# Retention attention, expert layer and closing layer on one core: another place for the split of the closing weights, and another order of work in the closing groups

## The chip, the cores and the metric

The kernel runs on one NeuronCore of a Trainium2 chip. The core has five engines that run side by side, each with its own queue in program order: TensorE (PE, matrix products into PSUM), VectorE (DVE), ScalarE (ACT), GpSimd (POOL, which cannot read PSUM) and SyncE (SP, which here issues nearly all DMAs). An instruction that has to wait holds up everything behind it on its own engine. The metric is the device time of one launch in microseconds (us), as the median of several runs.

## The reference

Three layers follow one another on 1536 rows of 512 columns (2 batches of 768 positions, 8 heads of 64).

```
attention:  blocks of 64 positions, masked by powers of lam, with a carried key-value state
experts:    P = exp(x @ w_gate - max), 8 times scaled by row sums and column sums
            out += P[:, e] * (relu(x @ w1[e]) @ w2[e])        for e in 0..7,  w1: 512x1024, w2: 1024x512
closing:    h = x @ w_in;  g = h - tanh(h);  out = g @ w_out   w_in: 512x2048, w_out: 2048x512
```

Everything is float32. The launch converts nothing but the layout: the closing weights w_in and w_out reach the kernel as 64-bit words, and the kernel turns them into float32 itself.

## The kernel before, in words

Every product in float32 is made of three products of reduced operands: each operand is split into a high part (a rounded copy, made by ACT with an fp32r output) and a low part (the source less the high part, made by DVE or POOL), and PE multiplies high by high, low by high and high by low. The helper is `split` (L174 to L178). The 512x512 products of first layers go by a scheme of seven products of sums of quarters instead of eight products of quarters; the quarters' sums are made on DVE and POOL beforehand, and the seven results are joined by DVE and ACT.

**The slots.** The expert layer runs in 64 slots (L819 to L868), each for a half of the rows and a sixteenth of all hidden columns. A slot has seven products into PSUM, `pal` four times, `pbl` once and `pbh` twice, each of six matmuls of 384 columns, and six `tiles` of the slot before, each of six matmuls of 512 columns. In the order of the code: product 1 into `pal`, which ACT copies to `sa` (L839); product 2 (`pbl`) and 5 (`pbh`); ACT copies `pbh` to `sa` (L845); product 6 onto `pal`, which must wait until L839 has read `pal`; ACT copies `pal` to `sb` (L848); three tiles of the slot before; product 7 onto `pal`, which must wait for L848; then DVE's sum `pah` (L855), the other three tiles, product 4 and product 3. `relu` (L674) makes the high part by ACT and the low part by DVE. Each tile is added by DVE to the accumulator `yacc` (L639). The PSUM bank of `pal` becomes the next slot's `pbh` when its `relu` is done.

Between these, four lists of small steps are run in every slot: `fd` after product 5, `fa` after L855, `fb` after the second three tiles, `fc` at the slot's end. They were filled by `put(list, slot, function, ...)` (L727 to L788). They hold the load (`w_load`, in `fc`), the quarter sums (`w_sum`, POOL, in `fa` of even slots) and the splits (`w1_split` in `fd` and `fa`, `w2_split` in `fb` of odd slots) of the next expert weights.

**The conversion of the closing weights.** The same lists hold `conv` (L560), which turns the 64-bit closing weights into float32 and stores their high and low parts in device memory (`wscr`) for later. There are 64 pieces of 128x256 words, 8 for each of the 8 parts of the layer, spread over slots 6 to 59; ten even slots take two pieces. For each piece: step 0 loads the words into `d` (`fc` of the slot before); step 1 (`fa`) has five DVE instructions (L576 to L583) and two of POOL (L584, L585), and writes the value `c`; step 2 (`fc`) has two of DVE (L587, L588) and then, at once, the split: ACT's high part `hl` (L176), POOL's low part (L178), and the store, which is put on a list and sent to SP when a later step calls `flush` in a later slot. A second piece of a slot uses `fd`, `fb` and the next slot's `fd` instead. The fourth piece of each part (p = 3) makes sums of quarters on POOL (L594, L595) and splits two of them at once, and in the next slot's `fa` two more (L607, L608). `block` (L553) rotates over three staging buffers `hl0` to `hl2`, `c` over five; a buffer `hl` of double width takes two pieces of w_out before its store.

**The closing groups.** From L936 on, 24 groups g run: three blocks of 512 rows times eight parts of 256 hidden columns. A group makes seven products of six matmuls of 256 columns into two PSUM banks `f0`, `f1` (each is one "unit" of 128x512), in the order 1, 2, 5, 6, 7, 3, 4. Between them `seconds` multiplies the finished units of earlier groups by w_out: unit 1 of group g-2 after product 2 and after product 6, unit 0 of group g-1 after product 3 and after product 4, two tiles at a time, each tile three matmuls of 512 columns. DVE and ACT join the products: `s1` (L942), DVE's L945 (after product 2; product 5 waits for it), L958, `s2` (L960, after product 6; product 7 waits for it), L978 and L980.

`unit(g, i, ...)` (L898) makes g = h - tanh(h) of a unit: ACT's square `t` (L908), ACT's `th` = tanh (L910), ACT's `q1`, `q2`, `mk` from `t` (L912 to L914); DVE's `w` = h*t (L916), `sub` = h - th (L918), the polynomial (L920, L921) and a predicated copy that chooses between polynomial and difference (L923); then ACT's high part (L926) and DVE's low part (L928). ACT and DVE take turns on the same PSUM bank in the order of the code, also where both only read.

**The turn from slots to groups.** At the end of the last slot the accumulators are transposed (`turn`, L681) and split for the first closing block by seven `x2_step`s on DVE and ACT (L713, L787), before the last `relu` and the last six tiles, which are spread over group 0.

Of the kernel before, what the change touches and what calls it, by code (L numbers as in the profile page):

```python
# [8 lines left out]
F32 = mybir.dt.float32  # L9
F32R = mybir.dt.float32r  # L10
BF16 = mybir.dt.bfloat16
I32 = mybir.dt.int32
# [17 lines left out]
NQ = FF // 512  # L30
# [25 lines left out]
def kernel(  # L56
# [494 lines left out]
        stores.append((now[0], tag, lambda: nc.sync.dma_start(out=wscr[q][:, :, o:o + m], in_=t.bitcast(F32))))  # L551

    def block(q, o, src):  # L553
        tag = f"hl{count[1] % 3}"
        t = staged(tag, 256, f"hl{q}_{o}")
        count[1] += 1
        split(t[:, 0], t[:, 1], src, nc.gpsimd)
        store(q, o, t, tag)

    def conv(u, i, j):  # L560
        q, p = 2 * u + i // 8, i % 8
        flush()
        if j == 0:
            d = cp.tile([128, NC64, 2], I32, tag="d", name=f"d{u}_{i}")
            nc.sync.dma_start(out=d.rearrange("p n t -> p (n t)"),
                              in_=wio[u].bitcast(I32)[:, i * 2 * NC64:(i + 1) * 2 * NC64])
            c0 = cp.tile([128, NC64], I32, tag="c0", name=f"c0_{u}_{i}")
            box[q, p] = [d, c0]
            return
        if j == 1:  # L570
            box[q, p].append(cq.tile([128, NC64], I32, tag=f"c1_{count[0] % 5}", name=f"c1_{u}_{i}"))
            count[0] += 1
        d, c0, c1 = box[q, p]
        hi, lo, val = d[:, :, 1], d[:, :, 0], c1.bitcast(F32)
        if j == 1:
            nc.vector.tensor_scalar(out=c0, in0=hi, scalar1=3, scalar2=0x40000000,  # L576
                                    op0=ALU.logical_shift_left, op1=ALU.bitwise_xor)
            nc.vector.tensor_scalar(out=c1, in0=hi, scalar1=-0x80000000, scalar2=None, op0=ALU.bitwise_and)
            nc.vector.scalar_tensor_tensor(out=c0, in0=c0, scalar=0x7FFFFFFF, in1=c1,
                                           op0=ALU.bitwise_and, op1=ALU.bitwise_or)  # L580
            nc.vector.tensor_scalar(out=val, in0=lo.bitcast(U32), scalar1=2.0 ** -52,
                                    scalar2=None, op0=ALU.mult)
            nc.vector.tensor_scalar(out=lo, in0=c0, scalar1=-0x800000, scalar2=None, op0=ALU.bitwise_and)  # L583
            nc.gpsimd.tensor_tensor(out=val, in0=val, in1=lo.bitcast(F32), op=ALU.mult)  # L584
            nc.gpsimd.tensor_tensor(out=val, in0=val, in1=c0.bitcast(F32), op=ALU.add)  # L585
        elif j == 2:
            nc.vector.tensor_scalar(out=lo, in0=hi, scalar1=0x7FFFFFFF, scalar2=None, op0=ALU.bitwise_and)  # L587
            nc.vector.scalar_tensor_tensor(out=val, in0=lo.bitcast(F32), scalar=thr, in1=val,  # L588
                                           op0=ALU.is_ge, op1=ALU.mult)
            if p < 3:  # L590
                block(q, (0, 256, 1536)[p], val)
            elif p == 3:
                a11, a22 = (box[q, k][2].bitcast(F32) for k in (0, 2))
                nc.gpsimd.tensor_tensor(out=a22, in0=val, in1=a22, op=ALU.add)  # L594
                nc.gpsimd.tensor_tensor(out=val, in0=a11, in1=val, op=ALU.subtract)  # L595
                block(q, WI[5], a22)
                block(q, WI[7], val)
            else:
                if p % 2 == 0:
                    box[q] = staged("hl", 512, f"hl{q}_{p}")  # L600
                ht, lt_ = (halves(box[q][:, t])[:, :, 128 * (p % 2):128 * (p % 2) + 128] for t in range(2))
                split(ht, lt_, odds(val), nc.gpsimd)
                if p % 2:
                    store(q, 1792 + 512 * (p // 2 - 2), box[q], "hl")
        elif p == 3:
            a11, a12, a22 = (box[q, k][2].bitcast(F32) for k in range(3))
            nc.gpsimd.tensor_tensor(out=a11, in0=a22, in1=a11, op=ALU.subtract)  # L607
            nc.gpsimd.tensor_tensor(out=a12, in0=a12, in1=a11, op=ALU.subtract)  # L608
            block(q, WI[6], a11)
            block(q, WI[3], a12)  # L610

# [100 lines left out]

    def x2_step(b, n, eng):  # L713
        for i in X2[n][0]:
            x2_block(b, i, eng)
        if X2[n][1]:
            x2_sum(b, X2[n][1], eng)

# [57 lines left out]
    for s in range(lo_, hi_):  # L776
        more = s % 2 == 0 and (s - lo_) // 2 * extra // ((hi_ - lo_) // 2) != ((s - lo_) // 2 + 1) * extra // ((hi_ - lo_) // 2)
        for steps in (((fc, s - 1), (fa, s), (fc, s)), ((fd, s), (fb, s), (fd, s + 1)))[:1 + more]:
            for j, (f, at_) in enumerate(steps):
                put(f, at_, conv, n // (nconv // NQ), n % (nconv // NQ), j)  # L780
            if n % 8 == 3:
                put(fa, at_ + 1, conv, n // (nconv // NQ), n % (nconv // NQ), 3)
            n += 1
    assert n == nconv
    for k in range(KT):
        put((fb, fc)[k // 2], NS - 1, turn, 0, k)
    for n in range(7):  # L787
        put(fc, NS - 1, x2_step, 0, n, nc.vector)  # L788


    def product(ps, s, i, start):
# [75 lines left out]
        pend = pbh  # L867
        run(fc[s])  # L868
    relu(pend, 0, 1)
    tiles(NS - 1, range(TPE // 2))  # L870


    glos = [xp2.tile([128, 512], F32R, name=f"gl{i}") for i in range(2)]
    units = [xp2.tile([128, 512], F32, name=f"un{i}") for i in range(6)]
# [23 lines left out]
    def unit(g, i, *steps):  # L898
        if not 0 <= g < ng:
            return  # L900
        v = 2 * g + i
        for step in steps:
            if step == "t":
                tmp[v] = {n: kinds[n][v % len(kinds[n])] for n in kinds}
            e = tmp[v]
            h = ph[g, i]
            if step == "t":
                nc.scalar.activation(out=e["t"], in_=h, func=ACTF.Square)  # L908
            elif step == "th":
                nc.scalar.activation(out=e["th"], in_=h, func=ACTF.Tanh)  # L910
            elif step == "q":
                nc.scalar.activation(out=e["q1"], in_=e["t"], func=ACTF.Square, bias=bias[:, 0:1])  # L912
                nc.scalar.activation(out=e["q2"], in_=e["t"], func=ACTF.Square, bias=bias[:, 1:2], scale=LEAD ** 0.5)
                nc.scalar.activation(out=e["mk"], in_=e["t"], func=ACTF.Relu, bias=bias[:, 2:3])  # L914
            elif step == "w":
                nc.vector.tensor_tensor(out=e["w"], in0=h, in1=e["t"], op=ALU.mult)  # L916
            elif step == "sub":
                nc.vector.tensor_tensor(out=h, in0=h, in1=e["th"], op=ALU.subtract)  # L918
            elif step == "p":
                nc.vector.scalar_tensor_tensor(out=e["w"], in0=e["q1"], scalar=Q1 * Q1, in1=e["w"], op0=ALU.add, op1=ALU.mult)  # L920
                nc.vector.scalar_tensor_tensor(out=e["q2"], in0=e["q2"], scalar=LEAD * Q2 * Q2, in1=e["w"],  # L921
                                               op0=ALU.add, op1=ALU.mult)
                nc.vector.copy_predicated(out=e["q2"], mask=e["mk"].bitcast(U32), data=h)  # L923
            elif step == "hi":
                gs[g, i] = [hh[i][g % 2].rearrange("p t n -> p (t n)")[:, 0:512], glos[i]]
                nc.scalar.activation(out=gs[g, i][0], in_=e["q2"], func=ACTF.Copy)  # L926
            else:
                nc.vector.tensor_tensor(out=gs[g, i][1], in0=e["q2"], in1=gs[g, i][0].bitcast(F32), op=ALU.subtract)  # L928
# [7 lines left out]
    for g in range(ng):  # L936
# [1 line left out]
        ph[g, 0], ph[g, 1] = f  # L938
        c11, c12, c21, c22 = f[0][:, 0:256], f[0][:, 256:512], f[1][:, 0:256], f[1][:, 256:512]
        cproduct(g, c21, 1, True)  # L940
        unit(g - 1, 1, "t")
        nc.scalar.activation(out=s1, in_=c21, func=ACTF.Copy)  # L942
        cproduct(g, c11, 2, True)
        unit(g - 1, 1, "w")
        nc.vector.tensor_tensor(out=c11, in0=c11, in1=s1, op=ALU.add)  # L945
        unit(g - 1, 1, "th")
        unit(g - 1, 0, "hi")
        if g == 0:
            tiles(NS - 1, (3,))
        elif g == 1:  # L950
            turn(2, 0)
            turn(2, 1)
        seconds(g - 2, 1, (0, 1))
        unit(g - 1, 1, "sub")
        unit(g - 1, 0, "lo")
        unit(g - 1, 1, "q", "p")
        cproduct(g, c12, 5, True)
        nc.scalar.activation(out=s1, in_=c12, func=ACTF.Copy)  # L958
        cproduct(g, c21, 6, False)
        nc.scalar.activation(out=s2, in_=c21, func=ACTF.Copy)  # L960
        unit(g - 1, 1, "hi")
        b, j = g // NG + 1, g % NG - 1
        if b < NBLK and j >= 0:
            if b == 2 and j == 0:
# [5 lines left out]
            turn(2, 2)  # L970
            turn(2, 3)
        seconds(g - 2, 1, (2, 3))
        unit(g - 1, 1, "lo")
        for n, (_, _, p) in enumerate(loads):
            if p >= 0 and p == g - 2:
                w2_load(n)
# [1 line left out]
        nc.vector.tensor_tensor(out=c22, in0=c21, in1=s1, op=ALU.add)  # L978
        cproduct(g, c12, 3, False)
        nc.vector.tensor_tensor(out=c12, in0=c12, in1=s2, op=ALU.add)  # L980
        unit(g, 0, "t", "th", "w", "sub", "q", "p")
        if g == 0:
            tiles(NS - 1, (5,))
            w2_load(2)
# [7 lines left out]
                turn(1, k)  # L992
        seconds(g - 1, 0, (2, 3))
    g = ng - 1
    unit(g, 1, "t", "w", "th")
    unit(g, 0, "hi")
    second(g - 1, 1, range(TPB))
    unit(g, 1, "sub")
    unit(g, 0, "lo")
    unit(g, 1, "q", "p")  # L1000
    second(g, 0, range(TPB), (0, 1))
    second(g, 0, range(TPB), (2,))
    unit(g, 1, "hi", "lo")
# [48 lines left out]
```

## Time and profile before

| | |
|---|---|
| median of 3 runs | 1367.54 us (1367.46 to 1367.87) |
| the profiled execution's own time | 1367.77 us |
| its span in the profile | 1366.0 us |
| PE busy | 1268.4 us (93%) |
| DVE busy | 1000.9 us (73%) |
| ACT busy | 588.9 us (43%) |
| POOL busy | 525.1 us (38%) |
| chain that ended last | PE 51%, DVE 28%, ACT 10% |

The span is what the profiler saw from the first to the last instruction; the profiled execution's own time is 1.8 us longer. Busy time is an average over stages with different limits: the attention stage runs to about 100 us, the slots to about 1057 us, the groups to the end. A busy PE is not PE at its peak, since overlapping matmuls are counted to their modelled ends. In the rows below a bracket gives the engine's idle time before an instruction and what ended it.

### The profile page before, as it was taken

The numbers are of one execution on the slowest core, as the hardware profiler recorded it, in microseconds if no ns is written. First come the engines' busy times: TensorE is split into PE (matmuls) and PEld (weight loads), VectorE is DVE, ScalarE is ACT, GpSimd is POOL, SyncE is SP. The second block draws the span as 40 slices with busy tenths as digits, with TensorE's granted clock in tenths as the row PEclk, the third lists the DMA queues.
The fourth block names the chain that finished last, engine by engine and source line by source line (L and its number), as shares of the span: only waits on it lengthen the run. The fifth ranks groups of instructions, "written<-read, shape, count | busy, mean of one in ns | idle before, by whom it ended". The sixth has DMA issues, their size and how long they took to land.

```text
span 1366.0 us, 20272 instructions
## 1 busy us (share of the span) xinstructions
PE 1268.4 (93%) x7450; PEld 1146.2 (84%) x7450; DVE 1000.9 (73%) x1916; ACT 588.9 (43%) x1191; POOL 525.1 (38%) x692
## 2 busy tenths in 40 slices
PE   8999998798999999999999998999999789899897
PEld 6889887798898988988898998998889677777776
DVE  7978876576667777777777677777765677877776
ACT  5553333233333333333333333333332477777665
POOL 4943435244444545445444445444540021121000
PEclk9999999899999999999999999999999899999999
DMA  9210112212232322222222322222232364371651
GB/s 330 89 31 32 54 62 86 77 62 77 77 97 67 115 86 85 70 78 70 85 70 70 124 85 90 73 78 78 85 132 91 134 226 144 140 255 62 223 200 62
DMA packets 59283, 141.84 MB, mean 104 GB/s; under 512 B 5808, under 2 KB 24752, under 8 KB 59184
## 3 DMA queue, kind: packets, MB, share of 16 engines
q1 hardware_dynamic: 59040, 140.55, 30.7%
q8 instruction: 58, 0.95, 0.3%
q14 instruction: 41, 0.34, 0.1%
q10 hardware_dynamic: 144, 0.00, 0.0%
HBM read 114.32 MB, written 26.21 MB: 103 GB/s over the span
## 4 chain that ended last, share of the span: by engine, by line
PE 51%; DVE 28%; ACT 10%; issue 5%; POOL 3%; DMA 1%; DVEq 0%; SPq 0%; ACTq 0%; POOLq 0%
PE yq L624 9%; PE yq L625 9%; PE yq L626 9%; PE pal L797 5%; PE pal L800 5%; PE pal L799 5%; DVE yacc L639 3%; DVE un_raw L921 2%; DVE un L920 2%; DVE gl L928 2%; ACT un L910 2%; PE pbh L799 2%; PE pbh L800 2%; PE pbh L797 2%; DVE h1l L677 2%
## 5 line engine op out<-in xcount | busy, mean ns | idle before, releaser
L639 DVE SCALAR_TENSOR_TENSOR yacc<-yq,prob,yacc 128x512 f32<-128x512 f32 x336 | 238.8, 746 | 92.7 <-PE yq L626 92.6
L797 PE MATMUL pal<-xsh,w1h 128*128 128x384 f32 x384 | 131.0, 341 | 45.6 <-ACT sa L839 39.5
L624 PE MATMUL yq<-w2h,h1h 128*128 128x512 f32 x384 | 148.2, 386 | 5.7 <-DVE yacc L639 5.7
L625 PE MATMUL yq<-w2l,h1h 128*128 128x512 f32 x384 | 147.7, 385 | 0.0
L626 PE MATMUL yq<-w2h,h1l 128*128 128x512 f32 x384 | 147.4, 384 | 0.0
L624 PE MATMUL yq<-w2h,h0h 128*128 128x512 f32 x384 | 147.2, 383 | 0.0
L625 PE MATMUL yq<-w2l,h0h 128*128 128x512 f32 x384 | 146.9, 382 | 0.0
L626 PE MATMUL yq<-w2h,h0l 128*128 128x512 f32 x384 | 146.6, 382 | 0.0
L176 ACT ACTIVATE hl<-c 128x256 fp32r<-128x256 f32 x88 | 38.8, 441 | 209.6 <-DVE c L588 140.8
L800 PE MATMUL pal<-xsh,w1l 128*128 128x384 f32 x384 | 126.8, 330 | 0.0
L799 PE MATMUL pal<-xsl,w1h 128*128 128x384 f32 x384 | 126.6, 330 | 0.0
L797 PEld LDWEIGHTS pal<-xsh,w1h 128*128 128x128 f32 x384 | 73.2, 191 | 61.7 <-ACT sa L839 48.0
L178 POOL TENSOR_TENSOR w1l<-wsum,w1h 128x256 fp32r<-128x256 f32 x124 | 90.4, 762 | 89.4 <-ACT w1h L176 89.4
L178 POOL TENSOR_TENSOR hl<-c,hl 128x256 fp32r<-128x256 f32 x88 | 64.8, 744 | 148.6 <-ACT hl L176 110.7
L584 POOL TENSOR_TENSOR c<-c,d 128x256 f32<-128x256 f32 x64 | 47.5, 742 | 149.1 <-DVE d L583 144.5
L676 ACT ACTIVATE h1h<-pah 128x384 fp32r<-128x384 f32 x64 | 31.4, 491 | 167.2 <-PE yq L625 163.4
L677 DVE SCALAR_TENSOR_TENSOR h0l<-pbh,h0h 128x384 fp32r<-128x384 f32 x64 | 35.6, 557 | 89.3 <-ACT h0h L676 89.3
L178 POOL TENSOR_TENSOR w2l<-wraw,w2h 128x512 fp32r<-128x512 f32 x64 | 83.7, 1326 | 7.0 <-ACT w2h L176 7.0
L624 PEld LDWEIGHTS yq<-w2h,h1h 128*128 128x128 f32 x384 | 73.8, 192 | 13.1 <-DVE yacc L639 5.9
L624 PEld LDWEIGHTS yq<-w2h,h0h 128*128 128x128 f32 x384 | 73.7, 192 | 10.8
L626 PEld LDWEIGHTS yq<-w2h,h1l 128*128 128x128 f32 x384 | 73.8, 192 | 10.7
L625 PEld LDWEIGHTS yq<-w2l,h0h 128*128 128x128 f32 x384 | 73.6, 192 | 10.7
(228 smaller groups left out, 3636.1 us busy)
## 6 DMA issues: line engine op xcount, KB each, us to landing
wraw<-in_w SPq DMA_DIRECT2D x64, 512.0 KB, 5.0
d<-in_wio SPq DMA_DIRECT2D x64, 256.0 KB, 5.8
wscr<-hl SPq DMA_DIRECT2D x56, 256.0 KB, 3.8
w1h<-wscr SPq DMA_DIRECT2D x18, 768.0 KB, 4.5
w1l<-wscr SPq DMA_DIRECT2D x18, 768.0 KB, 5.9
w2h<-wscr SPq DMA_DIRECT2D x18, 512.0 KB, 3.8
w2l<-wscr SPq DMA_DIRECT2D x18, 512.0 KB, 4.7
wscr<-hl SPq DMA_DIRECT2D x16, 512.0 KB, 5.3
```

What stands on the lines that cost most here:

```text
L176: nc.scalar.activation(out=hi, in_=src, func=ACTF.Copy)
L178: eng.tensor_tensor(out=lo, in0=src, in1=hi.bitcast(F32), op=ALU.subtract)
L584: nc.gpsimd.tensor_tensor(out=val, in0=val, in1=lo.bitcast(F32), op=ALU.mult)
L624: nc.tensor.matmul(out=yp, lhsT=hi, rhs=pairs(w2h[q][:, i]), start=i == 1, stop=False)
L625: nc.tensor.matmul(out=yp, lhsT=hi, rhs=pairs(w2l[q][:, i]), start=False, stop=False)
L626: nc.tensor.matmul(out=yp, lhsT=lo, rhs=pairs(w2h[q][:, i]), start=False, stop=i == 0)
L639: nc.vector.scalar_tensor_tensor(out=y, in0=yp, scalar=prob[:, c, q // 4:q // 4 + 1], in1=y, op0=ALU.mult, op1=ALU.add)
L676: nc.scalar.activation(out=hi, in_=ps, func=ACTF.Relu)
L677: nc.vector.scalar_tensor_tensor(out=lo, in0=ps, scalar=0.0, in1=hi.bitcast(F32), op0=ALU.max, op1=ALU.subtract)
L797: nc.tensor.matmul(out=ps, lhsT=w1h[q][:, ws], rhs=pairs(xh[:, k]), start=start and k == 0, stop=False, skip_group_check=True)
L799: nc.tensor.matmul(out=ps, lhsT=w1h[q][:, ws], rhs=pairs(xl[:, k]), start=False, stop=False, skip_group_check=True)
L800: nc.tensor.matmul(out=ps, lhsT=w1l[q][:, ws], rhs=pairs(xh[:, k]), start=False, stop=k == 1, skip_group_check=True)
```

## The change

**Slots.** The split of a piece moves from step 2 to a new step 3, which is put in `fa` of the next slot (for a second piece: of the slot of its step 2). For p = 3, step 3 has only the POOL sums L594 and L595; step 4, a slot later, splits these two and makes the POOL sums L607 and L608; step 5, another slot later, splits those. `flush` sends all waiting stores at steps 0 and 2. `block` rotates over four buffers, `c` over seven.

**The turn.** The seven `x2_step`s are interleaved with the last relu and the first three of the last tiles, after them in part. The low parts of three of the seven operands go to POOL.

**Groups.** Order and place of the unit's steps change; no instruction is added or removed. `th` follows `t` at once for both units. L942 (`s1`) comes ahead of the unit's `t`. For unit 0 the second polynomial step and the predicated copy move into the next group, on both sides of L945; unit 1's predicated copy moves behind L980, and its high and low part into the work on the next unit 0.

```diff
-        tag = f"hl{count[1] % 3}"
+        tag = f"hl{count[1] % 4}"
...
-        flush()
+        flush(j in (0, 2))
...
-            box[q, p].append(cq.tile([128, NC64], I32, tag=f"c1_{count[0] % 5}", name=f"c1_{u}_{i}"))
+            box[q, p].append(cq.tile([128, NC64], I32, tag=f"c1_{count[0] % 7}", name=f"c1_{u}_{i}"))
...
+        elif j == 3:
             if p < 3:
                 block(q, (0, 256, 1536)[p], val)
             elif p == 3:
                 a11, a22 = (box[q, k][2].bitcast(F32) for k in (0, 2))
                 nc.gpsimd.tensor_tensor(out=a22, in0=val, in1=a22, op=ALU.add)
                 nc.gpsimd.tensor_tensor(out=val, in0=a11, in1=val, op=ALU.subtract)
-                block(q, WI[5], a22)
-                block(q, WI[7], val)
...
-        elif p == 3:
+        elif j == 4:
             a11, a12, a22 = (box[q, k][2].bitcast(F32) for k in range(3))
+            block(q, WI[5], a22)
+            block(q, WI[7], val)
             nc.gpsimd.tensor_tensor(out=a11, in0=a22, in1=a11, op=ALU.subtract)
             nc.gpsimd.tensor_tensor(out=a12, in0=a12, in1=a11, op=ALU.subtract)
+        else:
+            a11, a12 = (box[q, k][2].bitcast(F32) for k in range(2))
             block(q, WI[6], a11)
             block(q, WI[3], a12)
...
-            x2_block(b, i, eng)
+            x2_block(b, i, nc.gpsimd if i in (3, 7, 4) else eng)
...
+            at_ = (at_, at_ + 1)[f is fc]
+            put(fa, at_, conv, n // (nconv // NQ), n % (nconv // NQ), 3)
             if n % 8 == 3:
-                put(fa, at_ + 1, conv, n // (nconv // NQ), n % (nconv // NQ), 3)
+                for j in (4, 5):
+                    put(fa, at_ + j - 3, conv, n // (nconv // NQ), n % (nconv // NQ), j)
...
-    for n in range(7):
-        put(fc, NS - 1, x2_step, 0, n, nc.vector)
...
-    tiles(NS - 1, range(TPE // 2))
-
+    for t, steps in enumerate(((0, 1), (2,), (3,))):
+        for n in steps:
+            x2_step(0, n, nc.vector)
+        tiles(NS - 1, (t,))
+    for n in (4, 5, 6):
+        x2_step(0, n, nc.vector)
```

In `unit`, step "q" becomes "q1", "q2", "mk" and step "p" becomes "w1", "p2", "cp", each one instruction. The group's loop:

```diff
         cproduct(g, c21, 1, True)
-        unit(g - 1, 1, "t")
         nc.scalar.activation(out=s1, in_=c21, func=ACTF.Copy)
+        unit(g - 1, 1, "t", "th", "q1")
         cproduct(g, c11, 2, True)
-        unit(g - 1, 1, "w")
+        unit(g - 1, 0, "p2")
         nc.vector.tensor_tensor(out=c11, in0=c11, in1=s1, op=ALU.add)
-        unit(g - 1, 1, "th")
+        unit(g - 1, 0, "cp")
+        unit(g - 1, 1, "w", "sub")
         unit(g - 1, 0, "hi")
+        unit(g - 1, 1, "q2")
...
         seconds(g - 2, 1, (0, 1))
-        unit(g - 1, 1, "sub")
         unit(g - 1, 0, "lo")
-        unit(g - 1, 1, "q", "p")
+        unit(g - 1, 1, "w1", "p2")
...
-        unit(g - 1, 1, "hi")
+        unit(g - 1, 1, "mk")
...
         seconds(g - 2, 1, (2, 3))
-        unit(g - 1, 1, "lo")
...
         nc.vector.tensor_tensor(out=c12, in0=c12, in1=s2, op=ALU.add)
-        unit(g, 0, "t", "th", "w", "sub", "q", "p")
+        unit(g - 1, 1, "cp")
+        unit(g, 0, "t", "th")
+        unit(g - 1, 1, "hi")
+        unit(g, 0, "q1", "q2", "mk", "w")
+        unit(g - 1, 1, "lo")
+        unit(g, 0, "sub", "w1")
```

The end behind the last group follows the same order.

## Rows read from the trace of the kernel before

**Rows 1.** Waits of PE, whole span: us in total, times, longest.
```profile
PE pal L797 <- ACT sa L839: 39.5, 29, 7.8
PE f L893 <- DVE f L945: 18.1, 22, 1.1
PE f L893 <- ACT sb L960: 7.6, 23, 0.8
PE pal L797 <- ACT sb L848: 6.1, 10, 1.9
PE yq L624 <- DVE yacc L639: 5.7, 1, 5.7
PE tr L684 <- DVE yacc L639: 3.9, 1, 3.9
```

**Rows 2.** Waits of all engines from 100 to 1055 us.
```profile
ACT hl L176 <- DVE c L588: 140.8, 55, 4.8
...
ACT hl L176 <- DMA wscr<-hl: 10.3, 1, 10.3
```

**Rows 3.** Timeline of PE, slots 22 and 23: start us, us, engine, line, what.
```profile
404.68 0.33 PE L797 MATMUL pal<-xph,w1h 128*128 128x384 f32 x1
...
419.27 0.33 PE L797 MATMUL pal<-xph,w1h 128*128 128x384 f32 x1
...
431.13 0.53 PE L797 MATMUL pal<-xsh,w1h 128*128 128x384 f32 x1
431.45 0.53 PE L799 MATMUL pal<-xsl,w1h 128*128 128x384 f32 x1
```

**Rows 4.** Timeline of ACT, slot 23.
```profile
422.50 0.42 ACT L176 ACTIVATE hl<-c 128x256 fp32r<-128x256 f32 x1 [3.50 <-DVE c L588]
...
429.84 0.47 ACT L848 ACTIVATE sb<-pal 128x384 f32<-128x384 f32 x1
```

**Rows 5.** Line L866, slots 5 to 62: count, durations in ns, first and last start.
```profile
L866 DVE TENSOR_TENSOR pbh<-pbh,sb x58: 554/556/561, 139.3 to 1041.2; 128x384 f32<-128x384 f32 x58
```

**Rows 6.** Timeline of DVE, slots 22 and 23.
```profile
414.18 0.33 DVE L576 TENSOR_SCALAR c<-d 128x256 int32<-128x256 int32 x1
...
432.81 0.79 DVE L576 TENSOR_SCALAR c<-d 128x256 int32<-128x256 int32 x1
```

**Rows 7.** Timeline of POOL, slot 23.
```profile
431.33 2.85 POOL L178 TENSOR_TENSOR w1l<-wsum,w1h 128x256 fp32r<-128x256 f32 x4 [0.48 <-ACT w1h L176]
```

**Rows 8.** Line L980, groups 1 to 23.
```profile
L980 DVE TENSOR_TENSOR f<-f,sb x23: 422/424/426, 1093.5 to 1347.4; 128x256 f32<-128x256 f32 x23
```

**Rows 9.** Chain that ended last, one group and the next start: start us, us, what.
```profile
1336.31 0.60 ACT un L908
...
1340.85 0.69 DVE un L916
...
1347.83 0.60 ACT un L908
```

**Rows 10.** Groups by line, 1300 to 1349 us: busy us, mean ns, idle before.
```profile
L916 DVE TENSOR_TENSOR un<-f,un 128x512 f32<-128x512 f32 x9 | 6.2, 685 | 5.8 <-ACT un L910 5.8
...
L910 ACT ACTIVATE un<-f 128x512 f32<-128x512 f32 x9 | 5.3, 594 | 6.3 <-DVE un L916 6.3
```

**Rows 11.** Busy time in the stretch of four groups: length, PE, PEld, DVE, ACT, POOL.
```profile
1300.00:1346.00 46.00, 41.60 (x267) 36.26 (x266) 35.68 (x60) 31.18 (x61) 0.00 (x0) 1.00 0.50 171
```

**Rows 12.** Timeline of PE, last group: one product, two tiles, the next tile.
```profile
1347.84 0.27 PE L893 MATMUL f<-x2h,w1h 128*128 128x256 f32 x1
...
1348.51 0.38 PE L652 MATMUL yp<-w2h,h0h 128*128 128x512 f32 x1
...
1349.81 0.38 PE L652 MATMUL yp<-w2h,h1h 128*128 128x512 f32 x1
```

**Rows 13.** Timeline of DVE at the turn.
```profile
1065.31 1.90 DVE L178 TENSOR_TENSOR x2l<-raw,x2h 128x512 fp32r<-128x512 f32 x3 [0.73 <-ACT x2h L176]
...
1067.59 2.06 DVE L639 SCALAR_TENSOR_TENSOR yacc<-yq,prob,yacc 128x512 f32<-128x512 f32 x3
```

More of the change, by code (lines that the diff above doesn't have):

```diff
@@ L910, in unit @@
                 nc.scalar.activation(out=e["th"], in_=h, func=ACTF.Tanh)
-            elif step == "q":
+            elif step == "q1":
                 nc.scalar.activation(out=e["q1"], in_=e["t"], func=ACTF.Square, bias=bias[:, 0:1])
+            elif step == "q2":
                 nc.scalar.activation(out=e["q2"], in_=e["t"], func=ACTF.Square, bias=bias[:, 1:2], scale=LEAD ** 0.5)
+            elif step == "mk":
                 nc.scalar.activation(out=e["mk"], in_=e["t"], func=ACTF.Relu, bias=bias[:, 2:3])
@@ L918, in unit @@
                 nc.vector.tensor_tensor(out=h, in0=h, in1=e["th"], op=ALU.subtract)
-            elif step == "p":
+            elif step == "w1":
                 nc.vector.scalar_tensor_tensor(out=e["w"], in0=e["q1"], scalar=Q1 * Q1, in1=e["w"], op0=ALU.add, op1=ALU.mult)
+            elif step == "p2":
                 nc.vector.scalar_tensor_tensor(out=e["q2"], in0=e["q2"], scalar=LEAD * Q2 * Q2, in1=e["w"],
                                                op0=ALU.add, op1=ALU.mult)
+            elif step == "cp":
                 nc.vector.copy_predicated(out=e["q2"], mask=e["mk"].bitcast(U32), data=h)
@@ L994 @@
     g = ng - 1
-    unit(g, 1, "t", "w", "th")
+    unit(g, 1, "t", "th", "q1")
+    unit(g, 0, "p2", "cp")
+    unit(g, 1, "w", "sub")
     unit(g, 0, "hi")
+    unit(g, 1, "q2", "mk")
     second(g - 1, 1, range(TPB))
-    unit(g, 1, "sub")
     unit(g, 0, "lo")
-    unit(g, 1, "q", "p")
+    unit(g, 1, "w1", "p2", "cp")
     second(g, 0, range(TPB), (0, 1))
```

## The prediction

> **What bounds the kernel now.** I read the waits of TensorE first, because TensorE is busy 93% of the span and a gain must come out of its idle time. The reader is to see that two stages hold nearly all of it [rows 1]: in the slots product 6 waits for ScalarE's L839 (39.5 us, 29 times) and product 7 for L848 (6.1 us); in the groups product 5 waits for VectorE's L945 (18.1 us, 22 times) and product 7 for L960 (7.6 us). Two single waits of 5.7 and 3.9 us lie at the turn between them.
>
> What a wait costs is more than its idle time, so I read it from the pace. A slot in which nothing waits takes 419.27 - 404.68 = 14.59 us [rows 3]. L866 ends each slot's TensorE work; from its first to its last start, 57 slots take 901.9 us, 15.82 each [rows 5]. 57 * 14.59 = 831.6, so the slots lose **70.3 us**, against 45.6 us of idle time. The rest is the clock: in slot 23, after a wait, matmuls of 384 columns start 0.32 us apart, which is 1.2 GHz [rows 3].
>
> Why L839 is late shows on ScalarE: it had stood 3.50 us before the `hl` split, which waited for L588, and L839 came right behind [rows 4]. Over the slots that is 140.8 us in 55 waits [rows 2]. ScalarE's queue is in order, so a split at the slot's end holds L839 until VectorE, which runs up to 3.2 us into the next slot (422.48 against 419.27), has done L588. Waits up to about 2 us are covered by products 2 and 5; the rest reaches TensorE.
>
> In the groups the chain of waits hardly meets TensorE. It alternates between ScalarE and VectorE, with a period of 1347.83 - 1336.31 = 11.52 us [rows 9]; over 22 groups it is 11.54 [rows 8]. Part of it is turn-taking on one PSUM bank: `w` needs only `t`, but waits for `th` (5.8 us), and `th` of unit 1 waits for `w` (6.3 us) [rows 10].
>
> **The change part by part.**
>
> *Slots.* The split now stands in `fa`, after L848 and L855, a slot behind its L588. Nothing ScalarE needs there is still to come: L588 and the POOL sums were issued a slot, or at least three tiles, earlier. L839 and L848 then have only TensorE and the relu in front of them. No instruction is added; ScalarE is 43% busy. VectorE keeps its order. The moved low parts (POOL, some 0.71 each [rows 7]) now stand before the next piece's L584 in POOL's queue, where POOL waits for VectorE anyway. SP gets each store one list earlier, behind `w_load` and ahead of the load of `d`; that load has most of a slot before L576 needs it. Four staging buffers and seven `c` cover the longer lives: a block's buffer comes round after four slots, or three for the last of a part.
>
> One place gets worse. Twice (slots 38 and 58) the sixth and seventh piece of a part share a slot, and both splits fall into one `fa`, where they use the same double buffer. ScalarE must then wait for the first one's POOL work (four w1l of 2.85 us in all, three low parts of 0.71 [rows 7]) and its store; three relus and two splits queue behind it, and the next slot's L839. The nearest row is the one wait of this kind now, 10.3 us [rows 2]. Bounds 0 and 10.3 for each; much of a slot covers it, so I take 4.5, half-clock included: 9 us, and 1 for the rest. Gain 70.3 - 10 = **60 us**; bounds 20 (both rivals on the slots below) and 70.
>
> *The turn.* The tile that waited 5.7 us stood behind eleven VectorE instructions of the seven steps and three sums into `yacc`; now it needs only four of them. But product 5 still waits for L945, behind all steps. Three low parts leave VectorE for POOL (3 took 1.90 us [rows 13]), and the tile (1.30 us, as six matmuls of 512 columns [rows 12]) runs before that wait, not after it: 3.2 us. At the second wait the tile's sum stands behind three unit steps, not five: 2 * 0.7 [rows 10] = 1.4. Sum 4.6, and some half-clock time: **5 us**, bounds 0 and 10.
>
> *Groups.* Per group TensorE needs seven products at 1348.51 - 1347.84 = 0.67 and four pairs of tiles at 1349.81 - 1348.51 = 1.30 [rows 12]: 4.69 + 5.20 = **9.89 us**. That is the floor. VectorE is busy 35.68 / 4 = 8.92 us a group, ScalarE 31.18 / 4 = 7.80 [rows 11]. In the new order I walk VectorE's loop from L980's end: unit 1's copy (about 0.7, as L916) runs beside `t` and `th` (1.1 us together [rows 9, 10]), so about 0.4 is idle before `w`; then `w`, unit 1's low part, `sub`, L920, L921, L945, copy, `w`, `sub`, low part, L920, L921 follow with inputs ready, since ScalarE is always one or two steps ahead. Only the two pairs L920 to L921 depend directly (0.1 each). 8.92 + 0.4 + 0.2 = 9.5 us: just under TensorE. From product 3's end L945 is then done after 0.42 (L980) + 1.15 + 3 * 0.6 + 0.8 + 0.6 + 0.42 = 5.2 us; TensorE reaches product 5 after three pairs of tiles and three products, 3 * 1.30 + 3 * 0.67 = 5.9. Product 7 has a pair of tiles (1.30) between itself and product 6, in which ScalarE must do L958 and L960 (under 0.4 each, no wait behind them). So the waits on L945 and L960 go, and TensorE is next. I take 9.9: 22 * (11.54 - 9.9) = **36 us**, bounds 0 (the turn-taking stays) and 36.3. The end behind the last group goes by the same order: 1 us, bounds 0 and 2. The weights for a group are loaded two groups ahead, so a shorter group does not meet them.
>
> Sum: 60 + 5 + 36 + 1 = 102. The profiled execution took 1367.77 us, 0.23 over the median, so 1367.77 - 102 - 0.2 = 1265.6: **1266 us**.
>
> **Rivals.**
>
> *A: VectorE and POOL collide in the slots.* L576 took 0.33 us alone and 0.79 while POOL's w1l ran [rows 6, 7]. POOL's low parts now fall nearer to step 1. If two of its instructions are held by 0.46 in each of 54 slots and `pal`'s low part, which frees the next `pbh`, is late by that, 54 * 0.92 = 50 us return: 1316; if half the slots have cover, **1290**. For: slots with two pieces leave VectorE 3.2 us behind. Against: the others have room.
>
> On this collision the Trainium skill, "SBUF — State Buffer", section "Who interferes with whom", says that a VectorE instruction which also takes the second port, or has two inputs in SBUF, and a GpSimd instruction shut each other out for a whole instruction. The trace agrees (0.79 for 0.33).
>
> *B: VectorE becomes the bound in the groups.* 9.5 against 9.89 is a thin margin. With 1.1 us more a group (one low part held by POOL, one ScalarE step late) the period is 10.6: 22 * 0.7 = 15 us back, **1281**.
>
> *C: the split's wait moves instead of going.* ScalarE might stand in `fa` for buffers or stores as long as it does now for L588, and half of both gains stay away: **1316**. Against: a buffer comes round after three slots at the earliest, and a store of this size has landed within one.
>
> *D, slower: SP's queue.* Stores now stand ahead of the load of `d` and wait for POOL, which may wait for `w_sum`'s data. If `d` is late, step 1 is, then the banks. One such stall cost 10.3 us [rows 2]; from 102 / 10.3 = 10 slots of 54 on it eats the whole gain, and with 14 the kernel takes **1410**. Against: `d` is sent almost a slot early.
>
> *E: the double buffer of slots 38 and 58 costs nothing*, and the turn gives 8: **1253**.
>
> **How the numbers follow.** Forecast 0.62 (1257 to 1276), A 0.13, B 0.13, C 0.04, D 0.02, E 0.06. Range 1254 to 1290: it leaves out C, D, the worse half of A and a bit of E. A measurement of this kernel tells about 0.2% (2.7 us) from no change. All but D and a small part of C lie far below: faster 0.97, same 0.01, slower 0.02.
>
> **What would show it.** Right: the wait of `hl` for L588 gone, L866's mean pace at 14.6 to 14.8, with losses after slots 39 and 59 alone; L980's pace at 9.9, TensorE's waits on L945 and L960 near zero; the 5.7 us wait replaced by one for L945. Wrong: `pbh` waiting for h1l (A), a pace over 10.3 (B), `hl` waiting for stores or POOL in many slots (C), L576 waiting for DMA (D).

## The result and the profile after

The changed kernel takes **1291.22 us** (median of 4 runs, 1288.29 to 1292.51), 0.9436 of before (95% interval 0.9419 to 0.9453). The forecast was 1266 with a range of 1254 to 1290: the direction holds, but the gain is 76 us where 102 were forecast, and the time lies just above the range.

Where the gain came from is read as in the prediction, from the starts of one line of VectorE in the slots (L870 is L866 of before) and one in the groups (L992 is L980). Of after, slots 5 to 62 and groups 1 to 23:

```profile
L870 DVE TENSOR_TENSOR pbh<-pbh,sb x58: 549/557/564, 139.6 to 1005.8; 128x384 f32<-128x384 f32 x58
...
L992 DVE TENSOR_TENSOR f<-f,sb x23: 422/433/433, 1054.2 to 1272.3; 128x256 f32<-128x256 f32 x23
```

57 slots take 866.2 us against 901.9 [rows 5], 22 groups 218.1 against 253.9 [rows 8], and the way from the last L870 to the first of these L992, which is the turn with group 0, 48.4 against 52.3. By stage, with the forecast:

| stage | gain measured, us | forecast |
|---|---|---|
| slots | 35.7 | 60 |
| turn and group 0 | 3.9 | 5 |
| 22 groups | 35.8 | 36 |
| behind the last group (1366.0 - 1347.4 against 1290.7 - 1272.3) | 0.2 | 1 |

So nearly all that is missing is missing in the slots. They still lose 866.2 - 831.6 = **34.6 us** against the unstalled 14.59 each; the forecast left 10. The waits of after that answer to [rows 1], TensorE first, whole span:

```profile
PE pbh L801 <- DVE h1l L680: 17.5, 17, 2.2
PE pbl L801 <- DVE h0l L680: 4.4, 3, 2.9
PE f L901 <- DVE f L957: 3.5, 1, 3.5
PE tr L687 <- DVE yacc L642: 2.3, 1, 2.3
```

The waits on L839 and L848 (now L843, L852) and, but for the first group, on L945 (L957) are gone. In their place products 5 and 2 of a slot wait for VectorE's `relu`. Why VectorE is late shows one view further, in its own waits in the slots, to set beside [rows 2]:

```profile
DVE c L576 <- DMA d<-in_wio: 22.9, 13, 3.8
DVE c L578 <- POOL hl L178: 1.9, 3, 0.6
```

and ScalarE's, in the same stretch:

```profile
ACT hl L176 <- DMA wscr<-hl: 35.6, 5, 9.2
ACT hl L176 <- DVE c L588: 0.3, 1, 0.3
```

The 140.8 us for L588 are 0.3, as forecast. New are three things: step 1 of a piece waits for its load (22.9 us in 13 slots, none before), `hl` waits for its double buffer's store (35.6 for 10.3), and, in the groups by line, step 1 itself has become slower. L578 and L579 of before, busy us and mean ns:

```profile
L579 DVE SCALAR_TENSOR_TENSOR c<-c,c 128x256 int32<-128x256 int32 x64 | 31.0, 484 | 2.2
...
L578 DVE TENSOR_SCALAR c<-d 128x256 int32<-128x256 int32 x64 | 26.0, 406 | 4.8 <-POOL hl L178 4.8
```

and of after:

```profile
L579 DVE SCALAR_TENSOR_TENSOR c<-c,c 128x256 int32<-128x256 int32 x64 | 38.2, 597 | 2.2
L578 DVE TENSOR_SCALAR c<-d 128x256 int32<-128x256 int32 x64 | 36.5, 570 | 1.9 <-POOL hl L178 1.9
```

All five lines of step 1 together went from 132.4 to 155.0 us. Slot 27 shows why. The timeline of DVE in after (start us, us, engine, line, what):

```profile
466.66 0.50 DVE L576 TENSOR_SCALAR c<-d 128x256 int32<-128x256 int32 x1
467.08 0.88 DVE L578 TENSOR_SCALAR c<-d 128x256 int32<-128x256 int32 x1
467.99 0.84 DVE L579 SCALAR_TENSOR_TENSOR c<-c,c 128x256 int32<-128x256 int32 x1
468.87 0.35 DVE L581 TENSOR_SCALAR c<-d 128x256 f32<-128x256 uint32 x1
```

and POOL's in the same slot:

```profile
464.11 2.88 POOL L178 TENSOR_TENSOR w1l<-wsum,w1h 128x256 fp32r<-128x256 f32 x4 [4.57 <-ACT w1h L176]
466.95 1.60 POOL L178 TENSOR_TENSOR hl<-c,hl 128x256 fp32r<-128x256 f32 x2
469.67 0.74 POOL L584 TENSOR_TENSOR c<-c,d 128x256 f32<-128x256 f32 x1 [1.12 <-DVE d L583]
```

While POOL makes the two moved low parts, L578 and L579 take 0.88 and 0.84; L581 behind them starts 0.3 after POOL is done and takes 0.35.

The late load is seen on SP. What the `w_load` DMAs (L121) wait for, before (us in total, times, longest):

```profile
SPq L121 <- POOL w2l L178: 321.6, 30, 21.8
```

Mostly they wait until POOL has split what is in the buffer that they fill, and what stands behind them on SP waits too. SP's timeline in slot 26 before (x2: two DMAs):

```profile
470.07 0.81 SPq L121 DMA_DIRECT2D wraw<-in_w  x2
470.94 0.93 SPq L565 DMA_DIRECT2D d<-in_wio  x2
```

the same slot after:

```profile
442.30 0.81 SPq L121 DMA_DIRECT2D wraw<-in_w  x2
443.15 2.04 SPq L551 DMA_DIRECT2D wscr<-hl  x3
445.23 1.58 SPq L565 DMA_DIRECT2D d<-in_wio  x2
```

and the step 1 that needs the load, before:

```profile
478.51 0.33 DVE L576 TENSOR_SCALAR c<-d 128x256 int32<-128x256 int32 x1
```

and after:

```profile
451.69 0.31 DVE L576 TENSOR_SCALAR c<-d 128x256 int32<-128x256 int32 x1 [2.13 <-DMA d<-in_wio]
```

Before, the load was issued 478.51 - 470.94 = 7.6 us ahead of its use. The page of before has a median of 5.8 us from issue to landing for this load, so by the median 1.8 were to spare; load by load, 21 of the 64 landed only 0.2 to 2.4 us ahead of L576. After, three stores stand ahead of it and take 2.04 us to issue, VectorE is ready 7.3 us behind the first of the `w_load` DMAs (451.69 - 2.13 - 442.30), not 8.4, and the load lands 6.4 us behind its issue, not 5.8. L576 waits 2.13.

In slot 27 product 5 then waits 2.24 for h1l, but not all of that is the load's. ScalarE was late in slot 26 as well:

```profile
451.13 0.54 ACT L176 ACTIVATE hl<-c 128x256 fp32r<-128x256 f32 x1 [6.13 <-DMA wscr<-hl]
```

`relu` stands behind this `hl`. With the load in time (the first two runs below) product 5 of slot 27 still waits 1.4 us.

### The profile page after: what moved, and what is told of

Same layout as the page of the kernel before. It is cut to its first block, busy times and chain, and to the rows that moved or that the text cites. A ratio compares the mean times of both kernels' runs of the same rounds, so it can differ in the third digit from the quotient of the medians.

```text
span 1290.7 us, 20235 instructions
## 1 busy us (share of the span) xinstructions
PE 1248.2 (97%) x7450; PEld 1147.6 (89%) x7450; DVE 1017.7 (79%) x1913; ACT 590.4 (46%) x1191; POOL 532.3 (41%) x698
## 4 chain that ended last, share of the span: by engine, by line
PE 47%; DVE 13%; DMA 5%; POOL 4%; issue 2%; ACT 2%; SPq 1%; DVEq 0%; POOLq 0%; ACTq 0%
PE yq L627 5%; PE yq L628 5%; PE yq L629 5%; DMA d<-in_wio 5%; DVE yacc L642 3%; PE yp L655 3%; PE yp L656 3%; PE yp L658 3%; PE f L901 3%; PE f L904 3%; PE f L903 3%; PE pal L801 3%; PE pal L803 3%; PE pal L804 3%; PE pbh L801 2%
## 5 line engine op out<-in xcount | busy, mean ns | idle before, releaser
L801 PE MATMUL pal<-xsh,w1h 128*128 128x384 f32 x384 | 126.7, 330 | 0.0
L628 PEld LDWEIGHTS yq<-w2l,h0h 128*128 128x128 f32 x384 | 72.7, 189 | 10.3
L627 PEld LDWEIGHTS yq<-w2h,h0h 128*128 128x128 f32 x384 | 72.7, 189 | 10.3
L629 PEld LDWEIGHTS yq<-w2h,h0l 128*128 128x128 f32 x384 | 72.6, 189 | 10.4
L628 PEld LDWEIGHTS yq<-w2l,h1h 128*128 128x128 f32 x384 | 72.7, 189 | 6.8
L849 ACT ACTIVATE sa<-pbh 128x384 f32<-128x384 f32 x64 | 31.5, 491 | 103.5 <-DVE pbl L847 87.5
L803 PEld LDWEIGHTS pal<-xsl,w1h 128*128 128x128 f32 x384 | 73.4, 191 | 4.2 <-DVE xsl L178 0.8
```

Source lines behind the costliest of these rows:

```text
L627: nc.tensor.matmul(out=yp, lhsT=hi, rhs=pairs(w2h[q][:, i]), start=i == 1, stop=False)
L628: nc.tensor.matmul(out=yp, lhsT=hi, rhs=pairs(w2l[q][:, i]), start=False, stop=False)
L629: nc.tensor.matmul(out=yp, lhsT=lo, rhs=pairs(w2h[q][:, i]), start=False, stop=i == 0)
L801: nc.tensor.matmul(out=ps, lhsT=w1h[q][:, ws], rhs=pairs(xh[:, k]), start=start and k == 0, stop=False, skip_group_check=True)
L803: nc.tensor.matmul(out=ps, lhsT=w1h[q][:, ws], rhs=pairs(xl[:, k]), start=False, stop=False, skip_group_check=True)
```

## The experiments

In all of them the slots' loss is that of the L870 of the kernel, first to last start of slots 5 to 62, less 831.6. Each is read from one trace. The slots of the changed kernel stand unaltered in two of the runs below and lose 35.1 and 33.6 there, so a difference of about 1 us says nothing. Theory **T** says the stores ahead of `d` on SP cost the missing 25 us; rival **A** (the prediction's) says that POOL's low parts hold VectorE's step 1.

### Undo the order on SP

```
-        flush(j in (0, 2))
+        flush()
```

> One line of the change taken back: the stores of the closing weights go to SP's queue only from an older slot, so behind the load of d, as before the change. Theory T (SP's order): in the changed kernel the load of d stands behind three stores that wait for POOL, L576 waits 22.9 us for it in 13 slots, h1l is late, product 5 of the next slot waits (17.5 us). It expects the wait of L576 for DMA under 3 us, the waits of pbh for h1l under 8 us, the slots' loss down from 34.9 us to 15 to 22 (slots 40 and 60 keep their 11.7), and a time of 1272 to 1280 us against 1291. Rival A (VectorE and POOL collide): the wait of L576 goes, but step 1's pieces still take 218 us in all against 192 before, h1l stays late in the same slots, 1287 to 1292.

Measured: 1281.13 us, ratio 0.9382 (0.9363 to 0.9401); wait of L576 for DMA 3.4 us, `pbh` for h1l 11.7, loss 854.6 - 831.6 = 23.0. The second form issues the load first and the stores behind it:

```
-        flush(j in (0, 2))
         if j == 0:
...
             box[q, p] = [d, c0]
+            flush(True)
             return
+        flush()
```

> The load of d is issued first and the stores directly behind it, in the same slot. Theory T expects the same as from the kernel with the old order: wait of L576 under 3 us, pbh for h1l under 8 us, slots' loss 15 to 22 us, 1272 to 1280 us; and, since the stores leave a slot earlier than in the old order, ScalarE's 35.6 us of waits for stores stay as they are and do not grow. Rival A expects 1287 to 1292.

Measured: 1281.62 us, 0.9387 (0.9368 to 0.9406), the same picture: load waits 3.5 us, `pbh` 11.7, loss 22.6. ScalarE's waits for stores grew a little, 35.6 to 41.0. So T is right for 12 us of loss and wrong for the rest: the time is just over its upper end, and h1l is late in 11 slots though `d` is in 3 alone.

### Take POOL's low parts away

On top of the first form:

```
-        split(t[:, 0], t[:, 1], src, nc.gpsimd)
+        split(t[:, 0], t[:, 1], src, nc.gpsimd, (0,))
+        nc.scalar.activation(out=t[:, 1], in_=src, func=ACTF.Copy)
```

and likewise for the pieces of w_out.

> The old order of SP's queue, and the low parts of the closing weights are written by ScalarE as a copy of the values (wrong numbers, the closing block's output is not the reference's) where POOL subtracted: 88 instructions of 0.8 us leave POOL, 88 of 0.4 come to ScalarE. Against the kernel with the old order alone: Rival A (collision) expects step 1's pieces on VectorE down from 218 to about 195 us in all, the remaining pbh waits for h1l gone and 10 to 15 us less time. Theory T expects the same time within 4 us, since with d in time VectorE's extra 26 us are covered.

Measured: 1264.86 us, 0.9257 (0.9230 to 0.9284), 16.3 us below the kernel with the old order alone; steps 1 and 2 take 185.0 us for 219.5, the loss is 839.5 - 831.6 = 7.9, `pbh` waits 3.6. That is a little more than A's numbers; T expected the same time within 4 us. But POOL also had 69 us less to do here (464.9 against 534.0), and ScalarE's waits for stores fell too (40.5 to 28.6), so this run alone doesn't tell a collision from a late POOL or from late stores.

### Other slots for the pairs

```
-        more = s % 2 == 0 and (s - lo_) // 2 * extra // ((hi_ - lo_) // 2) != ...
+        more = s in (10, 16, 22, 26, 32, 36, 42, 48, 54, 56)
```

> The extra pieces of slots 38 and 58 are moved to slots 36 and 56, so that the sixth and seventh piece of a part no longer share a slot; else the changed kernel. If the shared double buffer causes the loss of slots 40 and 60 (11.75 us together), it goes nearly whole: loss of those two slots under 2 us together, ScalarE's waits of hl for stores down from 35.6 us by the two longest (9.2 and 7.4), time 1279 to 1284 us. If the loss is that of two pieces in one slot whatever pieces they are, it moves to slots 37 or 38 and 57 or 58, and the time stays at 1288 to 1292.

Measured: 1279.49 us, 0.9379 (0.9354 to 0.9403). Slots 40 and 60 lose nothing, ScalarE's waits for stores fall from 35.6 to 19.1, the loss from 34.6 to 24.5. The other three waits, in slots 12, 26 and 46, stay. Some of the loss moved on (slot 57 now loses 3.9, waiting for h1l behind a late load). Together with the load first:

> Both single edits together: the load of d ahead of the stores, and the extra pieces in slots 36 and 56 in place of 38 and 58. Alone they took 11.9 and 10.0 us from the slots' loss of 34.9. If their causes are separate, about 13 us of loss are left and the time is 1268 to 1273 us against 1291 (0.929 to 0.932 of before). If the shared double buffer was late only because SP was, the two don't add: 1278 or more.

Measured: 1268.86 us, 0.9282 (0.9268 to 0.9296); loss 842.8 - 831.6 = 11.2. The two causes are separate to about 1 us: 34.6 - 12.0 - 10.1 would be 12.5.

### Move the third step, leave nothing out

On top of both:

```
-            put(fa, at_, conv, n // (nconv // NQ), n % (nconv // NQ), 3)
+            put(fb, at_, conv, n // (nconv // NQ), n % (nconv // NQ), 3)
```

> As the kernel with both edits, and the third step of each piece (split on ScalarE, low part on POOL, store) is moved within the slot from ahead of step 1 of the next piece to behind the second batch of tiles, so behind that step 1; nothing is left out. Theory A (the collision of POOL's low parts with step 1 on VectorE costs the second half of the loss) expects step 1 and 2 down from 217 to 190 to 200 us in all, the waits of pbh for h1l under 5 us, the slots' loss 13 to 5 or less, 1261 to 1266 us. The rival, that the gain of the run without POOL's low parts came from POOL having 71 us less to do (POOL's own lateness, not the collision), expects POOL as late as before and 1268 to 1273.

Measured: **1261.01 us**, 0.9225 (0.9212 to 0.9239). Loss 834.6 - 831.6 = 3.0; `pbh` waits 1.2 us in two slots. Step 1's five lines take 131.3 us, as before the change, with POOL as busy as in the changed kernel (531.6 us against 532.3). (Steps 4 and 5, the splits of a part's fourth piece, stay in `fa`.) So the gain doesn't need a POOL with less to do, and step 1 is slower because of what runs beside it. In slot 27, which was shown for after, step 1 has POOL beside it only for the rest of w1l. DVE:

```profile
457.94 0.53 DVE L578 TENSOR_SCALAR c<-d 128x256 int32<-128x256 int32 x1
458.38 0.34 DVE L580 TENSOR_SCALAR c<-d 128x256 int32<-128x256 int32 x1
458.75 0.43 DVE L581 SCALAR_TENSOR_TENSOR c<-c,c 128x256 int32<-128x256 int32 x1
```

POOL:

```profile
455.39 2.87 POOL L178 TENSOR_TENSOR w1l<-wsum,w1h 128x256 fp32r<-128x256 f32 x4 [4.55 <-ACT w1h L176]
460.01 0.74 POOL L586 TENSOR_TENSOR c<-c,d 128x256 f32<-128x256 f32 x1 [1.75 <-DVE d L585]
```

(L578, L580 and L581 here are L576, L578 and L579 of after.)

The time, though, isn't settled for A. The edit also moves ScalarE's high part and the store, and ScalarE's waits for stores fall from 24.2 us in the kernel with both edits to 11.2 here. In that kernel they made `relu` late on their own. Slots 26 and 27:

```profile
447.42 0.58 ACT L176 ACTIVATE hl<-c 128x256 fp32r<-128x256 f32 x1 [6.94 <-DMA wscr<-hl]
448.41 0.56 DVE L682 SCALAR_TENSOR_TENSOR h0l<-pbl,h0h 128x384 fp32r<-128x384 f32 x1 [1.48 <-ACT h0h L681]
453.52 0.43 PE L803 MATMUL pbh<-xsh,w1h 128*128 128x384 f32 x1 [1.38 <-DVE h1l L682]
```

Step 1 is hardly held there: its five instructions take 2.0 us for one piece and 1.7 for the other. In slots 32 and 33 of the same kernel it is held, to 3.6 us, and nothing else is late:

```profile
534.87 2.49 POOL L178 TENSOR_TENSOR hl<-c,hl 128x256 fp32r<-128x256 f32 x3
535.02 0.86 DVE L580 TENSOR_SCALAR c<-d 128x256 int32<-128x256 int32 x1
535.92 0.84 DVE L581 SCALAR_TENSOR_TENSOR c<-c,c 128x256 int32<-128x256 int32 x1
542.86 0.43 PE L803 MATMUL pbh<-xsh,w1h 128*128 128x384 f32 x1 [1.50 <-DVE h1l L682]
```

Of the 7.4 us of `pbh` waits in that kernel, 2.0 are of the first kind (slots 27 and 47) and 2.0 of the second (33, 39, 57). The other 3.4 are mixed; three of these four waits have a load 0.6 to 1.3 us late as well. The later place of the third step is worth 11.2 - 3.0 = 8.2 us; how that divides between A and ScalarE's waits for stores no run shows.

One place later still, with `fc` for `fb`:

> As the kernel with the third step behind the second tiles, but with the third step one place later still, at the end of the slot, so that POOL's low parts run in the first part of the next slot, where VectorE has no step 1, but in odd slots the subtractions w1l and in all slots the sum that frees pbl's bank. Theory A expects step 1 of the pieces below 200 us as there, L178 on VectorE (0.70 alone) longer, and a loss between 3 and 8 us: 1261 to 1266. If it matters only that POOL's low parts do not stand ahead of POOL's own part of step 1, and not what VectorE does beside them, the loss is 3 to 4 us as there: 1260 to 1262.

Measured: 1260.42 us, 0.9251 (0.9236 to 0.9267, beside runs of before of 1362.4 in the median), loss 3.1. Step 1 takes 131.9 us; step 2's L590 42.6 for 31.9 in the changed kernel, the split of w1l 0.710 for 0.712. ScalarE doesn't wait for stores any more. A had expected a longer split of w1l, which didn't come; POOL's low parts now hold step 2, and the loss stays as it is: here a held instruction showed in the time only where a bank waited behind it.

### The change in halves

The slots of the change alone (the diff's hunks from L554 to L611 and L784 to L788), and all its other hunks alone:

> The change's slots alone; the turn and the closing groups as before. The traces of before and after give 35.2 us for the slots: 0.972 to 0.976 of before (1327 to 1333 us). If a gain in the slots is eaten at the turn, where the next wait stands at a fixed point, it is less: over 0.980.

> The change's turn and closing groups alone; the slots as before. The traces give 39.9 us: 0.969 to 0.973 of before (1323 to 1329 us). Pace of the groups 10.1 us as in the changed kernel, product 5 of group 0 waiting about 3.5 us for L957.

Measured: 1331.50 us, 0.9740 (0.9723 to 0.9757), and 1326.56 us, 0.9698 (0.9677 to 0.9718). 0.0260 + 0.0302 = 0.0562 against 0.0564 for the whole: the halves add, and nothing of the slots' gain is eaten at the turn. (The groups' pace in the second is 9.9 us, as in the changed kernel; the 10.1 of the expectation was wrong.)

### The turn

```
-            x2_block(b, i, nc.gpsimd if i in (3, 7, 4) else eng)
+            x2_block(b, i, eng)
```

> The changed kernel with one part taken back: the low parts of operands 3, 7 and 4 of the first closing block on VectorE, not on POOL. The prediction said that POOL takes 1.9 us from VectorE's chain at the turn. If so, the wait of product 5 of group 0 grows from 3.5 to 5 or 6 us and the time is 2 us longer, which this comparison hardly tells from 1291; the trace decides. Rival: POOL's instructions there take 1.2 to 1.4 us each and hold VectorE's sums, so taking them away costs nothing: wait of 3.5 us or less.

Measured: 1292.07 us. Product 5 of group 0 waits 4.7 us for 3.5, and the turn with group 0 is 1.4 us longer in the trace; between what either side expected. Then, on top of the kernel of 1261.01:

```
-    for n in (4, 5, 6):
-        x2_step(0, n, nc.vector)
...
         if g == 0:
+            for n in (4, 5, 6):
+                x2_step(0, n, nc.vector)
             tiles(NS - 1, (3,))
```

> The kernel with d first, the extra pieces in other slots and the third step behind the second tiles, and one edit more at the turn: steps 4 to 6 of the first closing block's operands are issued in group 0 behind L957, not ahead of it. In the changed kernel product 5 of group 0 waits 3.5 us for L957, because ScalarE's copy of product 1 stands behind the three high parts of these steps, the last of which waits 2.5 us for VectorE's sum. Expected: that wait under 0.5 us, some of it back at product 6, which now needs step 4; the turn 2 to 4 us shorter and the rest as without this edit: 1257 to 1260 us (0.919 to 0.9215 of before). If the steps are the limit wherever they stand, product 6 waits as long as product 5 did, and it stays at 1261.

Measured: **1258.90 us** (1257.21 to 1259.83), 0.9240 (0.9226 to 0.9254) beside runs of before of 1362.4. Product 5's wait fell to 2.0, not under 0.5, and the turn with group 0 is 4.4 us shorter in the trace (975.3 to 1024.9 against 973.8 to 1019.0). The two kernels ran in different groups of runs, with a before 4.6 us apart, and the ratios stand the other way round (0.9240 and 0.9225), so which kernel is faster isn't shown; that the turn is shorter rests on one trace of each.

## Why the prediction was wrong

**Slots, the failed step.** It is this one: "SP gets each store one list earlier, behind `w_load` and ahead of the load of `d`; that load has most of a slot before L576 needs it." The place in a list was taken for a time. SP issues the load only when the `w_load` ahead of it has its buffer: in slot 26 that was 7.6 us before its use, half a slot, with 1.8 to spare. Three stores took 2.04. I had set it at nothing; it cost 34.6 - 22.6 = 12.0 of the 34.6 us, by the run with the load first.

**Slots, the rest of the 10 us.** The shared double buffer was right in its place (slots 40 and 60, behind 38 and 58) and a little small: 9 forecast, 22.6 - 11.2 = 11.4 by the two runs. But it was short in slots 12, 26 and 46 too, for 6.1 to 6.7 us each, where nothing was forecast: the store that it waits for stands behind `w_load` on SP like the load. Rival A was taken as an alternative with a chance of 0.13, at 25 or 50 us. It happened in part. Its price for one instruction was right (0.46 forecast; L578 took 0.88 for about 0.33), but most of the hits are covered: once the others are mended, A and these three further waits for stores cost 11.2 - 3.0 = 8.2 us together. How much of that is A's stays open; the waits in which step 1 alone was late are 2.0 of 7.4 us. 3.0 stay, 1 was forecast. 12.0 + 11.4 + 8.2 + 3.0 = 34.6.

On A's rule, the Trainium skill, "SBUF — State Buffer", section "Who interferes with whom", also says that the order of issue decides who is blocked. Slot 27 of after agrees: POOL's instruction came first (466.95 against 467.08), and VectorE's L578 took 0.88.

**Rival D** had the right mechanism and a price some ten times too high. 13 loads were late, but by 22.9 / 13 = 1.8 us each at a cost of 12.0 / 13 = 0.9, where it took 10.3 from a wait of another kind. So the slower side, which needed 10 stalls of that size, was never near.

**Rival C**'s waits for stores came too (35.6 us), but only as those of the double buffer; the four single buffers never waited for theirs. (C's 1316 is a slip: half of 60 and 36 is 48, which gives 1314.) **E** was wrong, **B** too: the groups keep TensorE's pace.

**Turn.** 3.9 for 5: the low parts on POOL brought 1.4 for 1.9, and the new wait for L957 came as named. ScalarE's queue adds to it: the copy that L957 needs (L953) stands behind three high parts of steps 4 to 6, the first of which waits 2.54 us for a sum of VectorE's. ACT and DVE of after:

```profile
1030.72 1.77 ACT L176 ACTIVATE x2h<-raw 128x512 fp32r<-128x512 f32 x3 [2.54 <-DVE raw L712]
1032.40 0.37 ACT L953 ACTIVATE sa<-f 128x256 f32<-128x256 f32 x1
1032.80 0.43 DVE L957 TENSOR_TENSOR f<-f,sa 128x256 f32<-128x256 f32 x1 [0.69 <-ACT sa L953]
```

With these steps behind L957, in the kernel of 1258.90 us, the copy is done early, and L957 starts right behind VectorE's own sums:

```profile
996.08 0.36 ACT L953 ACTIVATE sa<-f 128x256 f32<-128x256 f32 x1
999.27 0.42 DVE L957 TENSOR_TENSOR f<-f,sa 128x256 f32<-128x256 f32 x1
```

Product 5 still waits 2.0 of the 3.5 us there, so the larger part is VectorE's queue, as the prediction had it.

**Groups.** 9.91 us a group for 9.9 forecast. In the stretch of four groups that answers to [rows 11], TensorE has no idle time left:

```profile
1230.00:1270.00 40.00, 40.00 (x268) 37.35 (x267) 35.51 (x62) 31.55 (x64) 0.00 (x0) 1.00 0.61 207
```

**The range** left out a middle: A, D and the double buffer each as a whole story, none of them small and all at once. Three partial costs of 8 to 12 us came together.

## What to carry to other kernels

When an instruction is moved on a queue, read from the trace how long before its use each neighbour behind it is issued, and what is left after its usual flight; the position in the program's order is no time. When work moves to a quiet engine, look at what the neighbour that shares its port does in that stretch, and at what waits behind it. Rivals that can each happen in part belong in the sum as terms of their own. An edit that moves a step moves the parts of every engine in it: look at the waits of each before the gain is given to one of them.

## What the runs showed of the hardware

A wait of 3.5 us in group 0 cost more than itself. It shows in the stretch that ends with the first L992 (L994 in the other two kernels). In the changed kernel (length, PE, PEld, DVE, ACT, POOL, granted clock) the mean clock is 0.82:

```profile
1030.00:1039.28 9.28, 5.99 (x32) 5.55 (x33) 4.30 (x8) 2.81 (x6) 2.83 (x4) 0.82 0.00 0
```

In the kernel of 1261.01 us, with the same wait, it is 0.66:

```profile
1000.00:1009.94 9.94, 7.22 (x32) 6.66 (x33) 3.75 (x7) 2.81 (x6) 2.83 (x4) 0.66 0.00 0
```

And with the wait cut to 2.0 us (the kernel of 1258.90 us) 1.00:

```profile
998.00:1004.07 6.07, 4.33 (x32) 4.14 (x33) 4.12 (x8) 2.71 (x5) 2.98 (x4) 1.00 0.00 0
```

The same 32 matmuls keep TensorE busy for 5.99, 7.22 and 4.33 us. Why the same wait cost more in the second trace than in the first isn't shown. A mean between 0.5 and 1 is a stretch that was partly at 1.2 GHz: in after the matmuls of 256 columns start 0.11 us apart right behind the wait, and 0.21 apart half a us later.

That the collision of VectorE and POOL is nearly free where nothing waits behind it was new too: 42.6 - 31.9 = 10.7 us more on one line of step 2, and a loss of 3.1 us, as with the third step one place earlier (3.0).
